# The last block of w_down, loaded in fifteen shares of 15 to 1 rows

## The chip, the core and the metric

The kernel runs on one core of one Trainium2 chip. The time is that of the device, in microseconds (us), for one execution of the whole program; three executions of the kernel before gave a median of 1309.13 us, from 1309.1 to 1309.35. A profile is one further execution, recorded by the hardware: its span runs from the first to the last instruction, and its times count from the start of that span. PE is the matrix engine (its weight loads are listed apart, as PEld), DVE the vector engine, ACT the scalar engine, POOL GpSimd. SP is the engine that issues nearly all transfers, and 16 DMA engines move them.

## What is computed

One decode step of a transformer block for two sequences, all in float32: a layer norm, attention of 32 heads against caches of 8192 keys and values, and a gated feed-forward part (SwiGLU).

```python
h = x + attention(layernorm(x), k_cache, v_cache, wq, wo)   # B=2, H=32, Sk=8192, Dh=128
g = silu(layernorm(h) @ w_gate)                             # D=512, F=1792
u = layernorm(h) @ w_up
h2 = h + (g * u) @ w_down                                   # w_down is 1792 x 512
```

## The kernel before, in words

The two caches are 537 MB of the 565 MB that the core reads, so the program is a long stream of loads with work beside it. SP issues every load in one fixed order, from the list `loads` (loop at line 603): `wq`, then for each of the 32 rounds a tile of keys and a tile of values (8 MB each), then `wo` in two transfers, `w_gate` in one and `w_up` in two, and last `w_down` in five. Before the first transfer into a buffer that was used before, SP waits until the last reader of that buffer is done (`after`, `freed`). `wd_t`, the place of `w_down`, is the buffer of the last value tile, so SP's wait ahead of `w_down` is for the last attention product (line 346). The five `w_down` transfers then follow each other with no wait between them.

`w_down` is loaded with row p of the on-chip tile holding the 14 rows p*14 to p*14+13 of the matrix, one after the other: 14 column blocks of 512 numbers. `WD` cuts these 14 blocks into groups of 4, 4, 3, 2 and 1; each group is one transfer over all 128 partitions with its own semaphore, `wd0` to `wd4`, counted to 16. The last, `wd4`, is 128 rows of 2 KB, 256 KB.

At the end of the program everything hangs on PE: for each of the 14 blocks `c` it does four matmuls (line 583) into the four quarters of the tile `f_ps` (shown as `bank` in the profile), and ahead of the first block of each group it waits for the group's semaphore. A float32 matmul counts as two MATMUL and two LDWEIGHTS rows in the profile, so the group of one block is 8 of each. When the last matmul is done, DVE and ACT each copy half of the result (lines 596 and 597), and SP and ACT each store half (line 610). SP then clears the semaphores and waits for the stores.

Every semaphore is taken one by one with `alone`; `landed` maps a transfer to its semaphore and the count that says that it has arrived, and `wait("tensor", ...)` puts that wait into PE's stream.

Of the kernel before, what the change touches and what calls it, by code (L numbers as in the profile page):

```python
# [9 lines left out]
P = 128  # L10
# [3 lines left out]
class Program:  # L14
# [16 lines left out]
    def wait(self, engine, *points):  # L31
        for s, value in points:
            if self.known[engine].get(s, 0) < value:
                self.known[engine][s] = value
                self.steps[engine].append(lambda e, s=s, v=value: e.wait_ge(s, v))  # L35

    def do(self, engine, fn, sem=None, by=1):

        if sem is None:
            self.steps[engine].append(fn)  # L40
            return None
        self.count[sem] += by
        self.steps[engine].append(lambda e: fn(e).then_inc(sem, by))
        return sem, self.count[sem]
# [8 lines left out]
def decode_block(nc, x, k_cache, v_cache, wq, wo, w_gate, w_up, w_down, out):  # L53
    B, _, D = x.shape
# [4 lines left out]
    FB = F // P  # L59
# [73 lines left out]
    wait, do = g.wait, g.do  # L133
# [6 lines left out]
    def alone(name):  # L140
        return g.sem(name)
# [3 lines left out]
    landed = {}  # L145
    freed = {}
    loads = []
# [43 lines left out]
        ))  # L191
    wd_t = v_last
    WD = ((0, 4), (4, 4), (8, 3), (11, 2), (13, 1))
    for e, (c, n) in enumerate(WD):
        loads.append((
            ("wd", 0), e,
            wd_t[:, c * D : (c + n) * D],
            w_down.rearrange("(p c) m -> p (c m)", p=P)[:, c * D : (c + n) * D],
            alone(f"wd{e}"),
        ))  # L200
    count = {}
    for item, e, dst, src, sem in loads:
        count[sem] = count.get(sem, 0) + 16
# [9 lines left out]
    p0 = do("gpsimd", lambda e: e.memset(ident, 0.0), s_pool)  # L213
# [8 lines left out]
    p0 = do("gpsimd", lambda e: e.memset(sides, 0.0), s_pool)  # L222
# [13 lines left out]
    def layernorm(src, ready):  # L236
        wait("vector", *ready)
        p = do("vector", lambda e: e.bn_stats(stats, src), s_dve)  # L238
        wait("vector", p)
        p = do("vector", lambda e: e.bn_aggr(mv, stats), s_dve)  # L240
        wait("vector", p)
        p = do("vector", lambda e: e.tensor_scalar(ve, mv[:, 1:2], EPS, None, op0=OP.add), s_dve)
        wait("gpsimd", p)
        p = do("gpsimd", lambda e: e.tensor_tensor(rstd, ve, mhalf, op=OP.pow), s_pool)
        wait("vector", p)
        p = do(
            "vector",
            lambda e: e.tensor_scalar(y, src, mv[:, 0:1], rstd, op0=OP.subtract, op1=OP.mult),
            s_dve,
        )  # L250
        normed = p
        wait("tensor", p, ident_done)
        for c in range(DC):
            p = do(
                "tensor",
                lambda e, c=c: e.transpose(yt[:, c, :], y.rearrange("b (p c) -> b c p", c=DC)[:, c, :], ident[:B, :B]),
                s_pe if c == DC - 1 else None,
            )
        return normed, p

    _, p = layernorm(xs, [(x_in, 16)])


    for t, value in (
# [6 lines left out]
        p0 = do("gpsimd", lambda e, t=t, value=value: e.memset(t, value), s_pool)  # L271
    wait("gpsimd", p1)
    p0 = do(
        "gpsimd",
        lambda e: e.affine_select(
            out=place,
            in_=place,
            compare_op=OP.not_equal,
            fill=1.0,
            base=0,  # L280
            pattern=[[-1, 32]],
# [8 lines left out]
    p = do("vector", lambda e: e.tensor_copy(xT, yt), s_dve)  # L290
# [10 lines left out]
    for n, (m, b) in enumerate((m, b) for m in range(0, MQ, 4) for b in range(B)):  # L301
# [3 lines left out]
        for c in range(DC):  # L305
            for k in range(2):
                p = do(
                    "tensor",
                    lambda e, ps=ps, c=c, k=k, m=m, b=b: e.matmul(  # L309
                        ps[HALF[k]],  # L310
                        xb[:, c * B + b, :],
                        wqv[:, c, k, m : m + 4, :],
                        start=(c == 0),
                        stop=(c == DC - 1),
                    ),
# [111 lines left out]
    for i in range(U):  # L427
        m, b = divmod(i, B)
        parts = 2
        n = NJ // parts  # L430
        wait("vector", q_done[m // 4 * B + b])
        for c in range(parts):
# [7 lines left out]
            if i and c == 1:  # L440
                recip(i - 1)
            wait("vector", mult)
            p = do(
                "vector",
                lambda e, kt=kt, s=scores[i % 2][:, c * n : (c + 1) * n]: e.tensor_reduce(s, kt, axis=AX.X, op=OP.add),  # L445
                s_dve,
            )
        freed["k", i] = p
        if i:
# [16 lines left out]
    p = do(  # L466
        "vector",
        lambda e: e.tensor_tensor(
            om,
            oT.rearrange("p h b -> p b h")[:, :, :, None].to_broadcast([P, B, H, NQ]),  # L470
            quarter[:, None, None, :].to_broadcast([P, B, H, NQ]),
            op=OP.mult,
        ),
        s_dve,
    )
    wait("tensor", p)
    for b in range(B):
        p = do(
            "tensor",
            lambda e, b=b: e.matmul(  # L480
                oq_ps[:, b, :], om[:, b].rearrange("p h q -> p (h q)"), fold, start=True, stop=True
            ),
            s_pe if b == B - 1 else None,
        )
    wait("scalar", p)
    p = do("scalar", lambda e: e.activation(oq.rearrange("p c b -> p b c"), oq_ps, AF.Copy), s_act)
    wait("tensor", p, zeroed)
    for c in range(H):
        for e_, (c0, n) in enumerate(WO):
            if c0 == c:  # L490
                wait("tensor", landed[("wo", 0), e_])
        t = c % 4
        p = do(
            "tensor",
            lambda e, c=c, t=t: e.matmul(
                wide[0][32 * t : 32 * t + B, :],
                oq[:, c, :],
                wo_t[:, c * D : (c + 1) * D],
                start=(c < 4),
                stop=(c >= H - 4),  # L500
            ),
# [4 lines left out]
    p = do("scalar", lambda e: e.activation(osb, wide[0], AF.Copy), s_act)  # L506
# [13 lines left out]
    def project_f(first, ps):  # L520
        for c in range(DC):
            for e_, (c0, n) in enumerate(WF):
                if c0 == first + c:
                    wait("tensor", landed[("wf", 0), e_])
            w = wf_t[:, (first + c) * F : (first + c + 1) * F]
            for t in range(4):
                p = do(
                    "tensor",
                    lambda e, c=c, t=t, w=w: e.matmul(
                        ps[32 * t : 32 * t + 32, :],  # L530
                        hT[:, c, :],
                        w[:, t * FQ : (t + 1) * FQ],
                        start=(c == 0),
                        stop=(c == DC - 1),
                    ),
                    s_pe if c == DC - 1 and t == 3 else None,
                )
        return p

    gate, up = wide[1][:, :FQ], wide[0][:, :FQ]  # L540
    p = project_f(0, gate)

    wait("tensor", h1_done)
    for t in range(4):
# [8 lines left out]
    p = do("scalar", lambda e: e.activation(sg, gate, AF.Sigmoid), s_act)  # L553
    wait("vector", p)
    sg_done = do("vector", lambda e: e.tensor_mul(sg, gate, sg), s_dve)
    p = project_f(DC, up)
# [4 lines left out]
    p = do(  # L561
        "vector",
        lambda e: e.tensor_mul(
            gu.rearrange("p (c j) -> p j c", c=FB),
            up.rearrange("p (j c) -> p j c", c=FB),
            sg.rearrange("p (j c) -> p j c", c=FB),
        ),
        s_dve,
    )
    gT = rest[:, D + 2 * FQ : D + 3 * FQ]  # L570
    wait("vector", p)
    p = do("vector", lambda e: e.transpose(gT, gu), s_dve)
# [3 lines left out]
    for c in range(FB):  # L576
        for e_, (c0, n) in enumerate(WD):
            if c0 == c:
                wait("tensor", landed[("wd", 0), e_])
        for t in range(4):  # L580
            p = do(
                "tensor",
                lambda e, c=c, t=t: e.matmul(  # L583
                    f_ps[32 * t : 32 * t + 32, :],
                    gT[:, c * 32 : (c + 1) * 32],
                    wd_t[:, c * D + COLS[t] * P : c * D + (COLS[t] + 1) * P],
                    start=False,
                    stop=(c == FB - 1),
                ),
                s_pe if c == FB - 1 and t == 3 else None,  # L590
            )
# [13 lines left out]
    rows = out.rearrange("b s d -> (b s) d")  # L605
# [55 lines left out]
```

## Time and profile before

| what | value |
|---|---|
| median of three executions | 1309.13 us (1309.1 to 1309.35) |
| span of the profiled execution | 1308.1 us |
| median less span: what lies around the span | about 1.0 us |
| DVE busy | 1131.1 us, 86% |
| PE busy | 433.8 us, 33% |
| ACT busy | 80.7 us, 6% |
| bytes moved | 564.79 MB, mean 432 GB/s |
| first `w_down` transfer issued | 1269.38 us |
| first matmul of the last block | 1305.95 us |

The profiled execution's own time is not listed apart from its span; it is read as the span and the 1.0 us around it. The row of DMA use is in the tenths of each of 40 slices of the span, and the chain of waits follows the work that ended last back from the last instruction, step by step, to what released it. A group row gives an operation, its output and inputs, and how many; the bracket at the end of a timeline row gives the engine's idle time before it and who ended it.

### The profile page before, as it was taken

How to read it: one execution, taken by the hardware profiler on the slowest of the kernel's cores; microseconds unless marked ns; L12 is line 12 of the kernel's file. 1: busy time of each engine (PE TensorE's matmuls, PEld its weight loads, DVE VectorE, ACT ScalarE, POOL GpSimd, SP SyncE). 2: the span in 40 equal slices, each digit the busy share in tenths (PEclk: the TensorE clock that was granted, in tenths of full speed). 3: DMA queues.
4: the chain of work that ended last, by engine and by line, in shares of the span. 5: the costliest groups of instructions: out<-in, count | busy, mean ns of one | idle time of the engine just before them, and what ended most of it. 6: DMA issues, size and time to landing. Idle time of an engine off the chain costs nothing.

```text
span 1308.1 us, 6717 instructions
## 1 busy us (share of the span) xinstructions
PE 433.8 (33%) x2956; PEld 135.8 (10%) x2956; DVE 1131.1 (86%) x246; ACT 80.7 (6%) x272; POOL 3.1 (0%) x15
## 2 busy tenths in 40 slices
PE   3633123333213333312333321333331233332177
PEld 1211001011001011000101100101100010110022
DVE  1999988899888889888889988888988888998841
ACT  0100000000000000000000000000000000000010
POOL 0000000000000000000000000000000000000000
PEclk9866566666556666556666655666655666665578
DMA  9999999999999999999999999999999999999998
GB/s 402 439 439 441 425 423 443 437 431 443 425 441 425 443 423 445 421 445 427 441 439 427 443 425 443 423 441 425 443 423 443 443 425 445 423 443 425 441 418 378
DMA packets 10965, 564.79 MB, mean 432 GB/s; under 512 B 1222, under 2 KB 1226, under 8 KB 1612
## 3 DMA queue, kind: packets, MB, share of 16 engines
q1 hardware_dynamic: 10948, 564.67, 99.7%
q8 instruction: 5, 0.08, 0.0%
q14 instruction: 4, 0.03, 0.0%
q10 hardware_dynamic: 8, 0.01, 0.0%
HBM read 564.66 MB, written 0.00 MB: 432 GB/s over the span
## 4 chain that ended last, share of the span: by engine, by line
DMA 54%; DVE 45%; PE 1%; SPq 0%; issue 0%; DVEq 0%
DMA kslot<-in_A_k_cache_dram 48%; DVE kslot L436 22%; DVE s L445 22%; DMA kslot<-in_A_v_cache_dram 3%; DMA kslot<-in_B_w_down_dram 3%; PE opart L346 1%; DVE gm L389 0%; SPq L603 0%; DVE r L415 0%; PE bank L583 0%; DVE m L453 0%; DVE kslot L596 0%; DVEq L35 0%
## 5 line engine op out<-in xcount | busy, mean ns | idle before, releaser
L436 DVE TENSOR_TENSOR kslot<-kslot,qsb 128x8192 f32<-128x8192 f32 x64 | 555.6, 8681 | 127.9 <-DMA kslot<-in_A_k_cache_dram 127.9
L445 DVE TENSOR_REDUCE s<-kslot 128x64 f32<-128x8192 f32 x64 | 555.2, 8675 | 0.1
L346 PE MATMUL opart<-vslot,pz 128*8 128x512 f32 x1984 | 283.8, 737 | 247.3 <-DMA vslot<-in_A_v_cache_dram 247.3
L338 PE MATMUL bank<-gm,nscale 1*64 1x1 f32 x64 | 11.8, 251 | 359.1 <-DVE gm L389 359.1
L346 PEld LDWEIGHTS opart<-vslot,pz 128*8 128x8 f32 x1984 | 55.1, 103 | 449.9 <-DMA vslot<-in_A_v_cache_dram 249.9
L336 PE MATMUL bank<-ident,m 128*1 128x128 f32 x64 | 18.8, 396 | 168.9 <-DVE m L453 168.9
L338 PEld LDWEIGHTS bank<-gm,nscale 1*64 1x64 f32 x64 | 9.1, 200 | 375.1 <-DVE gm L389 375.1
L358 PE MATMUL bank<-rdiag,osb 128*128 128x2 f32 x256 | 33.7, 254 | 25.7 <-ACT osb L422 25.7
L396 ACT ACTIVATE nb<-bank 128x1 f32<-128x1 f32 x32 | 5.5, 171 | 553.1 <-PE bank L339 553.1
L417 ACT ACTIVATE rdiag<-fold,r 128x8 f32<-128x8 f32 x32 | 9.6, 300 | 484.6 <-DVE r L415 484.6
L358 PEld LDWEIGHTS bank<-rdiag,osb 128*128 128x128 f32 x256 | 31.0, 191 | 55.4 <-ACT osb L422 55.4
L309 PE MATMUL wide<-vslot,osb 128*64 128x512 f32 x128 | 30.3, 638 | 17.2 <-DMA vslot<-in_A_wq_dram 17.2
L341 PE MATMUL bank<-rs,sides 128*128 128x1 f32 x64 | 18.7, 361 | 41.4 <-ACT pz L402 41.4
L402 ACT ACTIVATE pz<-s,nb 64x128 f32<-64x128 f32 x64 | 25.5, 399 | 1.4
L422 ACT ACTIVATE osb<-opart 128x512 f32<-128x512 f32 x32 | 19.1, 597 | 69.6 <-PE opart L346 69.6
L336 PEld LDWEIGHTS bank<-ident,m 128*1 128x1 f32 x64 | 2.7, 81 | 172.4 <-DVE m L453 172.4
L341 PEld LDWEIGHTS bank<-rs,sides 128*128 128x128 f32 x64 | 16.0, 310 | 44.2 <-ACT pz L402 44.2
L309 PEld LDWEIGHTS wide<-vslot,osb 128*64 128x64 f32 x128 | 10.7, 148 | 36.1 <-issue 36.1
L238 DVE BATCH_NORM_STATS2 ln_stats<-attn 2x6 f32<-2x512 f32 x1 | 0.7, 686 | 13.2 <-PE attn L508 13.2
L402 ACT ACTIVATION_READ_ACCUMULATOR pz<-s,nb 64x1 f32 x64 | 11.8, 184 | 0.0
L339 PE MATMUL bank<-gm,nscale 1*64 1x1 f32 x64 | 11.8, 251 | 0.0
L453 DVE TENSOR_REDUCE m<-s 128x1 f32<-128x128 f32 x32 | 9.2, 286 | 1.1
(65 smaller groups left out, 97.3 us busy)
## 6 DMA issues: line engine op xcount, KB each, us to landing
kslot<-in_A_k_cache_dram SPq DMA_DIRECT2D x2, 4096.0 KB, 35.6
vslot<-in_A_wo_dram SPq DMA_DIRECT2D x1, 5120.0 KB, 21.8
kslot<-in_B_w_gate_dram SPq DMA_DIRECT2D x1, 3584.0 KB, 31.6
kslot<-in_B_w_up_dram SPq DMA_DIRECT2D x2, 1792.0 KB, 37.4
vslot<-in_A_wo_dram SPq DMA_DIRECT2D x1, 3072.0 KB, 28.7
kslot<-in_B_w_down_dram SPq DMA_DIRECT2D x2, 1024.0 KB, 31.4
kslot<-in_B_w_down_dram SPq DMA_DIRECT2D x1, 768.0 KB, 33.8
kslot<-in_B_w_down_dram SPq DMA_DIRECT2D x1, 512.0 KB, 34.6
```

The source lines that it names most:

```text
L309: lambda e, ps=ps, c=c, k=k, m=m, b=b: e.matmul(ps[HALF[k]], xb[:, c * B + b, :], wqv[:, c, k, m : m + 4, :], start=(c == 0), stop=(c == D ...
L336: e.matmul(mrow, m1, ident, start=True, stop=True).then_inc(s_pe, 1)
L338: e.matmul(nb_ps[HALF[0]], nscale, gm[:, 0:1], start=True, stop=True)
L339: e.matmul(nb_ps[HALF[1]], nscale, gm[:, 1:2], start=True, stop=True).then_inc(s_pe, 1)
L341: e.matmul(den, sides.rearrange("p w a -> p (w a)"), rs, start=True, stop=True).then_inc(s_pe, 1)
L346: inst = e.matmul(opart[32 * t : 32 * t + 2 * W, :], pz[:, w, :], t_v[:, w * W * DH : (w + 1) * W * DH], start=(w < 4), stop=(w >= NW - 4),)
L358: inst = e.matmul(ot_ps, osb[:, a * DH : (a + 1) * DH], rdiag[:, a::W], start=(a == 0), stop=(a == W - 1))
L402: lambda e, k=k, h=h: e.activation(pz[h, :, k * W : (k + 1) * W], s[h].rearrange("p (w a) -> p w a", a=W), AF.Exp, bias=nb[h], scale=SCALE ...
L417: do("scalar", lambda e: e.activation(rdiag, diag, AF.Copy, scale=r))
L422: do("scalar", lambda e: e.activation(osb, opart, AF.Copy), s_act_pe)
L436: mult = do("vector", lambda e, kt=kt, qb=qb: e.tensor_tensor(kt, kt, qb, op=OP.mult), s_dve)
L445: lambda e, kt=kt, s=scores[i % 2][:, c * n : (c + 1) * n]: e.tensor_reduce(s, kt, axis=AX.X, op=OP.add),
```

## The change

The last group of `WD` is no longer one transfer. Its 128 partitions are cut into fifteen consecutive shares, `SHARES`, of 15, 14, 13, 12, 11, 10, 10, 9, 8, 7, 6, 5, 4, 3 and 1 partitions. Each is a transfer of its own, with its own semaphore `wdl0` to `wdl14`. PE waits for all fifteen ahead of the last block. The first four groups, the bytes and their places are as before.

```diff
     WD = ((0, 4), (4, 4), (8, 3), (11, 2), (13, 1))
-    for e, (c, n) in enumerate(WD):
+    wd_src = w_down.rearrange("(p c) m -> p (c m)", p=P)
+    for e, (c, n) in enumerate(WD[:-1]):
         loads.append((
             ("wd", 0), e,
             wd_t[:, c * D : (c + n) * D],
-            w_down.rearrange("(p c) m -> p (c m)", p=P)[:, c * D : (c + n) * D],
+            wd_src[:, c * D : (c + n) * D],
             alone(f"wd{e}"),
         ))
+    SHARES = (15, 14, 13, 12, 11, 10, 10, 9, 8, 7, 6, 5, 4, 3, 1)
+    assert sum(SHARES) == P
+    p0 = 0
+    for e, n in enumerate(SHARES):
+        rows = slice(p0, p0 + n)
+        p0 += n
+        cols = slice(WD[-1][0] * D, FB * D)
+        loads.append((("wd", 0), len(WD) - 1 + e, wd_t[rows, cols], wd_src[rows, cols], alone(f"wdl{e}")))
...
     for c in range(FB):
         for e_, (c0, n) in enumerate(WD):
             if c0 == c:
-                wait("tensor", landed[("wd", 0), e_])
+                for e_ in (e_,) if c < FB - 1 else range(e_, e_ + len(SHARES)):
+                    wait("tensor", landed[("wd", 0), e_])
```

On SP, the end of the stream of loads before; `kslot0` is the buffer that holds `w_down`, the sizes are partitions x numbers, and the waits are named by semaphore:

```order
L603 DMA kslot1<-in_B_w_up_dram 128x3584 x2
L603 DMA kslot0<-in_B_w_down_dram 128x2048 [waits pe]
L603 DMA kslot0<-in_B_w_down_dram 128x2048
L603 DMA kslot0<-in_B_w_down_dram 128x1536
L603 DMA kslot0<-in_B_w_down_dram 128x1024
L603 DMA kslot0<-in_B_w_down_dram 128x512
L610 DMA out_0_dram<-kslot1 2x256 [waits res]
```

And the same place on SP now, from the fourth `w_down` transfer on (shares of 4, 3 and 1 partitions and the store follow):

```order
L615 DMA kslot0<-in_B_w_down_dram 128x1024
L615 DMA kslot0<-in_B_w_down_dram 15x512
L615 DMA kslot0<-in_B_w_down_dram 14x512
L615 DMA kslot0<-in_B_w_down_dram 13x512
L615 DMA kslot0<-in_B_w_down_dram 12x512
L615 DMA kslot0<-in_B_w_down_dram 11x512
L615 DMA kslot0<-in_B_w_down_dram 10x512 x2
L615 DMA kslot0<-in_B_w_down_dram 9x512
L615 DMA kslot0<-in_B_w_down_dram 8x512
L615 DMA kslot0<-in_B_w_down_dram 7x512
L615 DMA kslot0<-in_B_w_down_dram 6x512
L615 DMA kslot0<-in_B_w_down_dram 5x512
```

One issue has become fifteen, in the same place, ahead of the store of the result; nothing else on SP has moved.

On PE, the end of the program before (`bank1` is `f_ps`):

```order
L583 MATMUL bank1<-kslot0,kslot1 32x128 [waits wd2]
L583 MATMUL bank1<-kslot0,kslot1 32x128 x11
L583 MATMUL bank1<-kslot0,kslot1 32x128 [waits wd3]
L583 MATMUL bank1<-kslot0,kslot1 32x128 x7
L583 MATMUL bank1<-kslot0,kslot1 32x128 [waits wd4]
L583 MATMUL bank1<-kslot0,kslot1 32x128 x3
```

And now:

```order
L595 MATMUL bank1<-kslot0,kslot1 32x128 [waits wd2]
L595 MATMUL bank1<-kslot0,kslot1 32x128 x11
L595 MATMUL bank1<-kslot0,kslot1 32x128 [waits wd3]
L595 MATMUL bank1<-kslot0,kslot1 32x128 x7
L595 MATMUL bank1<-kslot0,kslot1 32x128 [waits wdl8,wdl7,wdl9,wdl6,wdl10,wdl5,wdl11,wdl4,wdl12,wdl3,wdl13,wdl2,wdl14,wdl1,wdl0]
L595 MATMUL bank1<-kslot0,kslot1 32x128 x3
```

The matmuls stand as they did; ahead of the last block one wait has become fifteen. In the built program the fourteen added ones stand in seven wait instructions of two semaphores each, and the fifteenth, for `wdl0`, is on the first weight load itself.

## The prediction

> **What bounds the kernel now.** I read the page's DMA row first, then the chain that ended last, then the last microseconds. The page:
>
> ```profile
> span 1308.1 us, 6717 instructions
> DMA  9999999999999999999999999999999999999998
> DMA 54%; DVE 45%; PE 1%; SPq 0%; issue 0%; DVEq 0%
> ```
>
> The 16 DMA engines are never idle until the last slice, so the loads set the length; the change touches 256 KB of 565 MB, at the very end. Only what happens after the last bytes are asked for can move. The chain in order of time, its last steps (start, length, what):
>
> ```profile
> 1269.38 0.33 SPq L603
> ...
> 1270.69 34.58 DMA kslot<-in_B_w_down_dram
> 1305.27 0.04 issue
> 1305.32 1.10 PE bank L583 x24
> 1306.42 0.02 issue
> 1306.44 0.28 DVE kslot L596
> ```
>
> The chain enters PE with the fourth group (two blocks), issued at 1270.69 and landed at 1305.27. The last transfers are issued some 34 us ahead of their landing. The timeline shows where the fifth comes in:
>
> ```profile
> 1304.05 0.86 PE L583 MATMUL bank<-kslot 128*32 128x128 f32 x24 [0.77 <-DMA kslot<-in_B_w_down_dram]
> 1305.32 0.38 PEld L583 LDWEIGHTS bank<-kslot 128*32 128x32 f32 x16 [0.67 <-DMA kslot<-in_B_w_down_dram]
> 1305.95 0.16 PEld L583 LDWEIGHTS bank<-kslot 128*32 128x32 f32 x8 [0.26 <-DMA kslot<-in_B_w_down_dram]
> 1306.44 0.28 DVE L596 COPY kslot<-bank 64x128 f32<-64x128 f32 x1 [5.67 <-PE bank L583]
> 1306.75 0.34 SPq L610 DMA_DIRECT2D out_dram<-kslot  x1
> ```
>
> The weight loads of the last block begin at 1305.95, after 0.26 us without work because the fifth transfer was not there. Those 0.26 us are all that the transfer costs now: had it landed long before, PE would still begin at 1305.32 with the fourth group and reach the last block at about 1305.69. **The most that this change can win is therefore 0.26 us, 0.02%.** A measurement of this kernel can tell about 0.2%, 2.6 us, from no change.
>
> **Why a transfer lands late.** DMA use at the end, in windows of 0.1 to 0.3 us (the last two columns are the mean busy share of the 16 engines and the rate):
>
> ```profile
> core 0: us, PE busy (x) PEld busy (x) DVE busy (x) ACT busy (x) POOL busy (x), PEclk, DMA share, GB/s
> 1303.50:1303.80 0.30, 0.00 (x0) 0.00 (x0) 0.00 (x0) 0.00 (x0) 0.00 (x0) 1.00 1.02 403
> 1304.20:1304.40 0.20, 0.20 (x12) 0.20 (x9) 0.00 (x0) 0.00 (x0) 0.00 (x0) 1.00 0.33 133
> 1304.60:1304.90 0.30, 0.30 (x12) 0.04 (x4) 0.00 (x0) 0.00 (x0) 0.00 (x0) 1.00 0.33 130
> 1305.00:1305.10 0.10, 0.00 (x0) 0.00 (x0) 0.00 (x0) 0.00 (x0) 0.00 (x0) 1.00 0.37 143
> 1305.40:1305.50 0.10, 0.10 (x8) 0.10 (x12) 0.00 (x0) 0.00 (x0) 0.00 (x0) 1.00 0.11 41
> 1305.60:1306.00 0.40, 0.40 (x20) 0.14 (x12) 0.00 (x0) 0.00 (x0) 0.00 (x0) 1.00 0.00 0
> ```
>
> Until 1303.8 all sixteen are busy; from 1304.2 to 1305.1 the share is 0.33 to 0.37, some six of sixteen (0.375); the last stops by 1305.6. So most engines finish about 1304.2, a group of about six runs up to 1.4 us behind, and the slowest decides every landing. Dealing out the last rows unevenly could help if the late engines get fewer. The rows do not say which engines these are.
>
> **Row time.** Groups three to five reach PE at 1304.05, 1305.32 and 1305.95. Between the last two lies the fifth group, 8 rows of 2 KB on each engine if 128 rows fall evenly on 16: 0.63 us, 0.079 us a row. The fourth, of 4 KB rows, took 1.27 us, just twice that, so what a transfer adds besides its rows is about nothing when it is queued well ahead (twice 0.63 is 1.26). Bounds for that addition in a small transfer: below, 0.00 by these two; above, 0.36 us, the time from the last busy DMA engine (before 1305.6) to PE's start at 1305.95, if an engine had to see each arrival confirmed before its next row. I take a value near the lower bound, 0.01, since the sequence of five queued transfers is the nearest row; the upper one is a rival.
>
> **The change, term by term.** *Where the rows go.* A transfer of n rows seems to use n engines, one row each, for n below 16. The only small load in the trace, x (2 rows of 2 KB), seen in slices of 4 ns:
>
> ```profile
> GB/s 0 0 0 0 0 0 0 0 0 0 0 0 0 0 0 0 512 512 0 0 0 0 0 0 0 0 0 0 0 0 0 0 0 0 0 1 1 0 0 0
> DMA packets 4, 0.00 MB, mean 26 GB/s; under 512 B 2, under 2 KB 2, under 8 KB 4
> q10 hardware_dynamic: 4, 0.00, 7.0%
> ```
>
> Its two packets of 2 KB start within 8 ns of each other, and one lasts about 80, so they ran on two engines. Estimate from this: fifteen shares give the engine that takes part in all of them 15 rows, then 14, 14, 13, 12, 11, 10, 9, 8, 7, 5, 4, 3, 2, 1 and 0, where each had 8. [...]
>
> An early engine with 15 rows ends at about 1304.2 + 7 x 0.09 = 1304.8, still ahead of the late ones. The slowest late engine moves by between -8 and +7 rows: -0.63 to +0.55 us. The gain stops at 0.26, because the fourth group is what is late next. If late engines were spread at random over the stair, the slowest two or three would hardly all stand low; I take +0.2 us for the landing.
>
> *PE.* Seven wait instructions are added; the trace has five like them:
>
> ```profile
> L35 PEldq EVENT_SEMAPHORE  x5: 51/51/51, 1.5 to 1299.7; - x5
> ```
>
> Queued behind them on PE are the last 8 weight loads and matmuls, and DVE, ACT and the store wait for those. Seven by 51 ns, with a step between, are 0.36 to 0.42 us if the share that comes last is in the first of them; nothing if it is in the last. Waits already met could also be passed while PE waits for others. I take +0.2 us.
>
> *SP.* Fourteen more issues:
>
> ```profile
> L603 SPq DMA_DIRECT2D kslot<-in_B_w_down_dram x5: 327/428/2540, 1269.4 to 1271.2; - x5
> 0.74 0.54 ACTq L212 DMA_DIRECT2D xs<-in_A_x_dram  x1
> 1251.18 0.80 SPq L603 DMA_DIRECT2D vslot<-in_A_wo_dram  x2
> vslot<-in_A_wo_dram SPq DMA_DIRECT2D x1, 5120.0 KB, 21.8
> vslot<-in_A_wo_dram SPq DMA_DIRECT2D x1, 3072.0 KB, 28.7
> kslot<-in_B_w_gate_dram SPq DMA_DIRECT2D x1, 3584.0 KB, 31.6
> ```
>
> At 0.43 us (SP's) to 0.54 us (x, which went to few engines) they take 6.0 to 7.6 us of SP, which waits until 1306.75 for its next work, the store. They begin at 1271.2 and the last row's turn comes at about 1303.2, so 25 us cover them. But the fifth issue took 2.54 us, to 1273.7: something was full. The first wo transfer landed at 1251.18 + 21.8 = 1273.0, just before. If the limit counts rows waiting for an engine, the shares fit as rows drain: the busiest engine gets 15 rows and 15 completions where it had 8 and 1, 21 more; 8 rows and a completion leave with the second wo transfer (landed about 1251.55 + 28.7 = 1280.3), 9 more with w_gate (1257.1 + 31.6 = 1288.7), the rest by about 1291, 12 us ahead of need. **Cost nothing**, as long as that is the limit.
>
> *Code.* The added instructions could bring one more code fetch into the tail:
>
> ```profile
> q8 instruction: 1, 0.02, 2.1%
> ```
>
> That is the window from 1303.2 to 1306: one fetch, 2.1% of 16 engines over 2.8 us, 0.94 us of one engine. Seven instructions on PE and fourteen on SP may or may not start another; 0 to +0.94 us, taken as 0.
>
> The sum: landing +0.2, PE +0.2, SP 0, code 0: +0.4 on the profiled 1308.1, or 1309.5 beside the median of 1309.13. The bounds: -0.26 with nothing added, and 0.55 + 0.42 + 0.94 = +1.9.
>
> **Rivals.** *The stair fits the late engines* (they are those with few rows): then the landing gains its 0.26 and PE's waits give back some; 1308.9 to 1309.2. Six late engines against six places with 5 to 0 rows speak for it; nothing shows that they are the same six. Within 0.2% too.
>
> *The limit counts transfers, not rows.* When the fifth issue stood still, nine were in flight (2 of wo, 3 of w_gate and w_up, 4 of w_down), and it went on 0.3 us after the oldest had landed, less its own 0.43. Then each share waits for one landing: the first nine by that of the fourth group, 1305.27, so that the ninth is issued by about 1306.0 and the last six, at 0.43, by 1308.6. From the start of the final store's issue (1306.75) to the end of the span are 1.35 us; so the last share lands at 1308.2 + 1.35 = 1309.5 instead of 1305.9: +3.6, **1312.7**, slower. It decides if the cap is below some 20 in flight. Against it: the stop ended at 1273.7, 0.7 us after the landing where an issue takes 0.43; while the slowest engine's next row of the second wo transfer, 0.9 us (7.3 us by 8) after its last of the first at about 1272.7, ends at 1273.6, just ahead of it. Rows fit better.
>
> *Small transfers pay per piece.* If each share costs an engine the 0.36 above, the busiest has 15 x 0.44 = 6.6 us from about 1303.2, then 0.36: 1310.2 instead of 1305.95, +4.2, **1313.3**. Against it: the queued transfers of four and two KB rows show no such part. [...]
>
> *The shares do not spread* (128 rows on one engine: 10 us, about 1317): x speaks against it.
>
> **How the numbers follow.** Forecast 0.66, fitting stair 0.20: both within 0.2%. Transfers counted 0.07, per piece 0.05, not spread 0.01: slower. Faster by over 2.6 us has no mechanism here: 0.01. So faster 0.01, same 0.86, slower 0.13. The range takes the bounds of the first two cases, 1309.13 - 0.26 and + 1.9, with 0.1 for scatter below: 1308.7 to 1311.0; the slower rivals are the part left out.
>
> **What would show it.** Right: SP's fifteen issues end before 1292; PE's wait ahead of the last block is within half a microsecond of 0.26; DMA use falls in another shape after 1303.9 but ends by about 1306.2. Transfers counted: issues still running after 1300 and a store that waits for SP. Per piece: DMA share low but not zero for several us after 1305. Code: a second q8 packet in the window from 1303. Wrong altogether if the time moves by more than 2 us with none of these.

## The result, and the profile after

| | before | after |
|---|---|---|
| median, 12 executions each | 1309.40 us (1309.1 to 1309.66) | 1311.84 us (1311.45 to 1312.44) |
| ratio to before, 95% interval | | 1.002 (1.0012 to 1.0028) |
| span of the profiled execution | 1308.1 us | 1310.5 us |

The change costs 2.4 us. That is just under the 0.2% bound of the prediction, but the two sets of executions do not touch, and 1311.84 lies outside the range of 1308.7 to 1311.0. The spans differ by 2.34 us, so the traces hold it. Three executions in what follows (one of e5, the profiled one of e10, one of before beside r0, e1, e2 and e5) took 150 to 440 us longer than the others; the medians leave them out, and e17 repeats e10 for its trace.

The page of after:

```profile
span 1310.5 us, 6738 instructions
DMA  9999999999999999999999999999999999999998
DMA 52%; DVE 45%; SPq 2%; PE 1%; issue 0%; DVEq 0%
```

Nothing of the stream is seen to change; SP's queue enters the chain with 2%. The chain of after in order of time, its last steps (start, length, what):

```profile
1289.29 1.02 SPq L615
1290.31 0.04 issue
1290.36 17.45 DMA kslot<-in_B_w_down_dram
1307.81 0.35 issue
1308.15 0.62 PE bank L595 x8
1308.78 0.02 issue
1308.80 0.28 DVE kslot L608
```

Before, the last landing in the chain was that of the fourth group, at 1305.27; now it is that of a share, at 1307.81, though SP issued it at 1290.3, 17 us ahead. Behind it stand 0.35 us in which PE works through its waits. The timeline of after:

```profile
1305.47 0.38 PEld L595 LDWEIGHTS bank<-kslot 128*32 128x32 f32 x16 [0.83 <-DMA kslot<-in_B_w_down_dram]
1308.12 0.19 PEld L595 LDWEIGHTS bank<-kslot 128*32 128x32 f32 x8 [2.28 <-issue]
1308.15 0.60 PE L595 MATMUL bank<-kslot 128*32 128x128 f32 x8 [2.04 <-DMA kslot<-in_B_w_down_dram]
1308.80 0.28 DVE L608 COPY kslot<-bank 64x128 f32<-64x128 f32 x1 [8.11 <-PE bank L595]
```

PE's idle time ahead of the last block was 0.26 us and is 2.28 us. Its eight weight loads and matmuls then take 0.68 us to the copy (1308.12 to 1308.80) where they took 0.49. The window of after around them shows why; the third number from the right is the clock that PE is granted, as a share of full speed:

```profile
1308.00:1308.80 0.80, 0.60 (x8) 0.19 (x8) 0.00 (x0) 0.00 (x0) 0.00 (x0) 0.67 0.00 0
```

The trace's records of this clock have it fall from 1.0 to 0.5 at 1308.27, within the block. In before it is 1.0 from 1294.36 to 1308.01, and the last matmul is done by 1306.44.

Now the question is whether the bytes come late. The use of the 16 DMA engines in 40 slices of 1303 to 1308 us, 0.125 us each, in tenths; first before, then after:

```profile
DMA  9999999944334243321000000000000000001000
```

```profile
DMA  8967927552443333311000000000000000000000
```

Both rows fall below a tenth after the 19th slice: the bytes end at nearly the same place. The same in windows, after (the last two columns are DMA share and GB/s):

```profile
1305.40:1305.90 0.50, 0.43 (x16) 0.38 (x16) 0.00 (x0) 0.00 (x0) 0.00 (x0) 1.00 0.06 21
1305.90:1306.40 0.50, 0.22 (x8) 0.00 (x0) 0.00 (x0) 0.00 (x0) 0.00 (x0) 1.00 0.00 0
```

After 1305.9 no DMA engine moves data, and the last landing is at 1307.81. So the time does not pass in moving bytes but between the last byte and the word that it has arrived. The trace's records of the semaphores show how that word comes: each engine that takes part in a transfer adds one when its part is done. The last of these additions for each share of after, in us, with the number of engines that took part (it is the number of rows, as the prediction had it from x):

```
share (engines)   0(15)   1(14)   2(13)   3(12)   4(11)   5(10)   6(10)
last addition     1305.61 1305.80 1305.99 1306.17 1306.36 1306.54 1306.72
share (engines)   7(9)    8(8)    9(7)    10(6)   11(5)   12(4)   13(3)   14(1)
last addition     1306.89 1307.07 1307.26 1307.44 1307.63 1307.81 1307.16 1306.11
last row of w_down moved: 1305.89     last addition: 1307.81
```

Shares 0 to 12 step by 0.17 to 0.19 us: one engine, with 13 rows, that reports one share after another. Its rows need 0.086 us each, and it has moved them all by 1305.89. The reports fall behind the rows by some 0.1 us a share until they lag by 1.92 us; before, the one report lagged by 0.32 (last row 1305.58, landing 1305.90). They do not start level: the last row of the fourth group is moved at 1304.78 and its landing is at 1305.43, 0.65 us behind, where before it was 0.34 behind (1304.93 and 1305.27).

In the records of the DMA engines each row of a share is followed by a packet of 4 bytes, one for each report, that takes 9 ns. The last of these packets ends at 1305.90, just behind the last row. So the engines work off the reports at the pace of the rows; it is their arrival that comes 0.18 us apart.

The 2.34 us between the two traces, by place: last row 0.31 later, reports behind it 1.60 more (1.26 from the thirteen shares, 0.33 the lag that the fourth group has already), PE's waits 0.27, PE's slower last block 0.18, the rest -0.02.

### The profile page after: what moved, and what is told of

It reads as the page before. It is cut to its first block, busy times and chain, and to the rows that moved or that the text cites. A ratio compares the mean times of both kernels' runs of the same rounds, so it can differ in the third digit from the quotient of the medians.

```text
span 1310.5 us, 6738 instructions
## 1 busy us (share of the span) xinstructions
PE 433.4 (33%) x2956; PEld 135.6 (10%) x2956; DVE 1131.1 (86%) x246; ACT 80.7 (6%) x272; POOL 3.1 (0%) x15
## 4 chain that ended last, share of the span: by engine, by line
DMA 52%; DVE 45%; SPq 2%; PE 1%; issue 0%; DVEq 0%
DMA kslot<-in_A_k_cache_dram 48%; DVE kslot L447 22%; DVE s L456 22%; DMA kslot<-in_A_v_cache_dram 3%; SPq L615 2%; DMA kslot<-in_B_w_down_dram 1%; PE opart L357 1%; DVE gm L400 0%; DVE r L426 0%; PE bank L595 0%; DVE m L464 0%; DVE kslot L608 0%; DVEq L35 0%
```

## The experiments

The expectations use these letters. **C**: an engine's reports (completions) follow each other some 0.18 us apart, which is slower than short rows. **R**: the stair puts 13 to 15 rows on some engine where each had 8. **S**: a small transfer pays a price wherever it stands in the stream. Later: **P**, shares of neighbouring partitions slow what lands beside them (crowding); **N**, the number of transfers counts; **G**, only the added issue and the shifted program code count.

| label | last block loaded as | median | before beside it | ratio, 95% |
|---|---|---|---|---|
| r0_changed_again | as in after | 1312.08 | 1309.27 | 1.002 (1.001 to 1.003) |
| e1_one_semaphore | 15 shares, one semaphore | 1311.89 | 1309.27 | 1.0019 (1.0009 to 1.0028) |
| e2_eight_by_16 | 8 shares | 1310.82 | 1309.27 | 1.0011 (1.0001 to 1.002) |
| e5_stair_of_four | 60, 40, 20, 8 | 1309.92 | 1309.27 | 1.0005 (0.9995 to 1.0015) |
| e3_four_by_32 | 4 shares | 1310.16 | 1309.35 | 1.0006 (0.9996 to 1.0015) |
| e4_two_by_64 | 2 halves | 1310.17 | 1309.35 | 1.0006 (0.9997 to 1.0015) |
| e6_eight_by_16_one_semaphore | 8 shares, one semaphore | 1310.92 | 1309.35 | 1.0011 (1.0002 to 1.0021) |
| e7_shares_first_one_semaphore | 15 shares, ahead of the other groups | 1311.75 | 1309.35 | 1.0019 (1.001 to 1.0029) |
| e9_two_by_64_interleaved | every 2nd partition | 1309.53 | 1309.43 | 0.9999 (0.999 to 1.0008) |
| e16_four_by_32_interleaved | every 4th | 1309.40 | 1309.31 | 0.9995 (0.9979 to 1.0012) |
| e10_eight_interleaved_one_semaphore | every 8th, one semaphore | 1310.93 | 1309.43 | 1.0012 (1.0003 to 1.0021) |
| e17_eight_interleaved_again | the same | 1311.14 | 1309.31 | 1.0006 (0.9988 to 1.0024) |
| e11_fourth_group_in_two | whole; fourth group in two | 1309.23 | 1309.43 | 0.9998 (0.9989 to 1.0007) |
| e8_three_blocks_8_by_16 | last 3 blocks, 8 shares | 1312.92 | 1309.43 | 1.0027 (1.0017 to 1.0036) |
| e12_three_blocks_interleaved | the same, every 8th | 1312.52 | 1309.26 | 1.0022 (1.0013 to 1.0032) |
| e13_whole_block_first | whole, ahead of the other groups | 1309.63 | 1309.26 | 1.0002 (0.9993 to 1.0012) |
| e14_eight_interleaved_first | every 8th, ahead | 1311.01 | 1309.26 | 1.0012 (1.0002 to 1.0022) |
| e15_eight_by_16_first | 8 shares, ahead | 1310.63 | 1309.26 | 1.001 (1.0 to 1.0019) |

All edits below are against after, except that of e7, which is against before.

### The waits and the stair: r0, e1, e2, e6, e5

> The changed kernel once more, as the measure for the others on this chip. Expected +2.2 to +2.6 us against the kernel before. By its first trace: data of the last shares gone by 1306.0, the last share counted as landed at 1307.81, PE's last block at 1308.12 instead of 1305.95.

Measured 2.8 us above before, more than expected, where the first comparison had 2.4. The reports step as in after, by 0.17 to 0.20 us, and the last landing is at 1308.01.

One semaphore for all shares, and one wait of PE:

```diff
+    wdl = alone("wdl")
-        loads.append((("wd", 0), len(WD) - 1 + e, wd_t[rows, cols], wd_src[rows, cols], alone(f"wdl{e}")))
+        loads.append((("wd", 0), len(WD) - 1 + e, wd_t[rows, cols], wd_src[rows, cols], wdl))
...
-                for e_ in (e_,) if c < FB - 1 else range(e_, e_ + len(SHARES)):
+                for e_ in (e_,) if c < FB - 1 else (e_ + len(SHARES) - 1,):
```

> Fifteen shares as in the change, but all on one semaphore, and PE waits once, for the full count of 240. If PE's chain of waits costs what its trace shows (last landing 1307.81, last block 1308.12, where one wait takes 0.05), this wins 0.25 to 0.3 us of the change's loss, so +2.1 against before, and the last landing stays near 1307.8. If the waits were the main cost, +0 to +0.5. If the separate semaphores slow the landings, the landing itself comes early.

Measured 1311.89 beside 1312.08 on the same chip: the separate waits are worth some 0.2 us, no more, and the loss is 2.6 us where 2.1 were expected. The two sets of executions overlap, so the 0.2 us rest on the traces. The timeline of e1 shows PE starting 0.04 us after the last landing (1307.63) and still late:

```profile
1307.67 0.20 PEld L596 LDWEIGHTS bank<-kslot 128*32 128x32 f32 x8 [2.00 <-DMA kslot<-in_B_w_down_dram]
1308.39 0.28 DVE L609 COPY kslot<-bank 64x128 f32<-64x128 f32 x1 [8.03 <-PE bank L596]
```

The block again takes 0.72 us, so that part does not hang on the number of semaphores. It does not hang on the length of the wait either: e6 and e17 (below) have PE idle for 1.07 and 1.12 us ahead of the last block, and the block takes 0.72 and 0.49 us. In e17:

```profile
1307.80 0.16 PEld L595 LDWEIGHTS bank<-kslot 128*32 128x32 f32 x8 [1.12 <-DMA kslot<-in_B_w_down_dram]
1308.29 0.28 DVE L608 COPY kslot<-bank 64x128 f32<-64x128 f32 x1 [7.26 <-PE bank L595]
```

It goes with the granted clock. Where the clock stays at 1.0 over a last group of one block, the block takes 0.49 to 0.52 us (before, e3, e5, e9, e11, e16, e17); where the clock has fallen to 0.5 before or within it, 0.68 to 0.74 us (after, r0, e1, e2, e6). In after the fall comes 13.65 us after the rise, as it does in before. What makes it fall is not shown by any run.

Equal shares, without the stair:

```diff
-    SHARES = (15, 14, 13, 12, 11, 10, 10, 9, 8, 7, 6, 5, 4, 3, 1)
+    SHARES = (16, 16, 16, 16, 16, 16, 16, 16)
```

> Eight shares of 16 rows, one row on each of the 16 engines and one completion for each: every engine has 8 rows as before, but 8 completions instead of 1, and no stair. Theory C (an engine's completions go out one after another, about 0.18 us each, slower than rows of 0.086): the slowest engine lands 8 x 0.18 = 1.44 us after its fourth group instead of 0.63, +0.8, and PE's three added wait instructions +0.1 to 0.3: +0.9 to +1.1 us against before. Theory R (the loss is the stair: the late engine was given 13 rows): no loss here, -0.1 to +0.2. [...]

> Eight shares of 16 as before, on one semaphore with one wait on PE. The run with eight semaphores had its last landing at 1306.98 and PE's last block at 1307.09, so PE's waits cost it only 0.06 beyond the single wait's 0.05. Theory C: landing again near 1307.0, last block 0.05 later; within 0.1 us of the eight semaphores' time (+1.3 to +1.6 against before). If separate semaphores were what makes completions slow, the landing comes near 1306.

1310.82, and 1310.92 with one semaphore: 1.6 us above before, with 8 rows on every engine as there. R alone falls. The time is also above the 0.9 to 1.1 us that C gave for e2: its last landing is 1.08 us later than before's, not 0.8, and the granted clock adds 0.25 in the last block (0.74 instead of 0.49). In e2 the last additions of the eight shares step by 0.19 to 0.22 us (1305.57, .77, .99, 1306.19, .39, .59, .79, .98), while the last row was moved at 1305.50. C's step holds for equal shares too, and the fifteen shares cost about 1 us more because 13 reports stand on the slowest engine instead of 8.

```diff
-    SHARES = (15, 14, 13, 12, 11, 10, 10, 9, 8, 7, 6, 5, 4, 3, 1)
+    SHARES = (60, 40, 20, 8)
```

> A stair again, but of four transfers of 60, 40, 20 and 8 partitions: if these go to 15, 10, 10 and 8 engines, engines 0 to 7 get 11 rows, 8 and 9 get 10, 10 to 14 get 4, and 15 none; four completions at most on an engine. Theory C: completions hide behind rows (4, 4, 2 and 1 rows at 0.08 between them), so only 3 rows more on the late low engine, +0.24, and little for PE's waits: +0.2 to +0.6. Theory R with a high price for rows given to the late engine: 3 of the 5 rows added by the change, +1.1. Theory S: four transfers, +0.6.

1309.92, 0.65 above before: just above C's range, near the 0.6 of S, and well below the 1.1 of R. On how many engines the shares of 60, 40 and 20 rows land is not shown here; 15, 10 and 10 were my assumption.

### Fewer, larger shares: e3, e4

`SHARES` is `(32, 32, 32, 32)` in e3, 64 KB a share, and `(64, 64)` in e4; nothing else is changed.

> Four shares of 32 rows: 2 rows and one completion on each engine per share. Theory C as the first runs left it (completions go out one per 0.18 to 0.20 us on an engine, beside the rows and not in their way): 2 rows take 0.165, so the last landing is at most 0.1 to 0.2 us later than before's 1305.90; PE's wait +0.1. In all +0.1 to +0.4 us. Theory C-added (a completion adds 0.1 us to its engine's rows): +0.3 at the landing, +0.4 to +0.5 in all. Theory S (each transfer of 64 KB or less pays a fixed price, 1.1 us for 7 more in the run with 8): 3 more, +0.5.

> Two shares of 64 rows: 4 rows (0.32 us) and one completion on each engine per share. Theory C: a completion of 0.18 to 0.20 hides behind 4 rows, last landing within 0.1 us of before's 1305.90, one more wait on PE; +0.0 to +0.2 us. If issuing the added transfer brought its own price (a further code fetch near 1280 us stood in all four traces of changed kernels and not in that of before), +0.3 or more and the fourth group's landing later than 1305.27.

Both took 0.8 us more than before: a miss for C, which has next to nothing to give where each report has two or four rows to hide behind (0.17 and 0.35 us). In e4 it was the fourth group, untouched by the edit, that landed late: 1306.05 instead of 1305.27. Something slowed the bytes.

### Shares ahead of the other groups: e7

The loop over `SHARES` stands ahead of the loop over `WD[:-1]`, with one semaphore:

```diff
-    for e, (c, n) in enumerate(WD):
...
+    wdl = alone("wdl")
+    for e, n in enumerate(SHARES):
...
+    for e, (c, n) in enumerate(WD[:-1]):
```

> The fifteen shares are issued ahead of the four large groups instead of behind them, on one semaphore; the bytes, the stair and the 128 completions are the same. Theory C: the completions drain while the 3.75 MB of the large groups move, and nothing at the end waits for them; what is left is the stair, 13 rows instead of 8 for the late engine 3, 5 x 0.086 = 0.43 on every later landing, so the fourth group lands at 1306.2 to 1306.5 instead of 1305.90 for the whole, and PE then has 24 matmul rows to go instead of 8: in all +0.6 to +1.0 us against before, at least 1 us better than the shares last (+2.6 with one semaphore +2.4). If the price sits in the transfers wherever they stand (S), the loss stays at +2 or more.

1311.75: another miss for C. All rows of the shares were moved by 1298.4 and the last report came at 1300.3, yet the fourth group landed at 1307.44. The loss is not only a backlog of reports at the program's end. S says so, but not why.

### Which partitions a share takes: e9, e10, e16, e17

A share takes every second (fourth, eighth) partition instead of neighbours; sizes and numbers of transfers stay:

```diff
-        rows = slice(p0, p0 + n)
-        p0 += n
+        rows = slice(e, P, len(SHARES))
```

> Two transfers of 64 partitions again, but of every second partition (0, 2, 4 .. and 1, 3, 5 ..) instead of the lower and the upper half. [...] Theory C (completions of one engine's transfers go out one after another, whatever the partitions): as with the halves, 1310.0 to 1310.3, fourth group near 1306.0.

> Four transfers of every fourth partition, each with its semaphore, in place of the four of 32 neighbouring partitions that took 1310.16. Theory N (the number of transfers, so of completions, sets the loss; with two it is hidden, with eight 1.5 us): 1309.8 to 1310.3, as with neighbouring partitions. Theory P (neighbouring partitions set the loss up to where completions take over at eight): 1309.3 to 1309.7.

1309.53 for two and 1309.40 for four: the 0.8 us are gone, though issues, semaphores, waits and rows are as many as in e4 and e3. The windows show what they were. First e4 (neighbouring halves), then e9 (interleaved halves):

```profile
1303.70:1304.30 0.60, 0.00 (x0) 0.00 (x0) 0.00 (x0) 0.00 (x0) 0.00 (x0) 1.00 0.89 191
```

```profile
1303.70:1304.30 0.60, 0.00 (x0) 0.00 (x0) 0.00 (x0) 0.00 (x0) 0.00 (x0) 1.00 1.06 406
```

Then e3 (neighbouring quarters) and e16 (interleaved quarters):

```profile
1303.70:1304.30 0.60, 0.01 (x1) 0.01 (x1) 0.00 (x0) 0.00 (x0) 0.00 (x0) 1.00 0.76 164
```

```profile
1303.70:1304.30 0.60, 0.60 (x24) 0.53 (x24) 0.00 (x0) 0.00 (x0) 0.00 (x0) 1.00 0.41 160
```

Read share and rate together. A DMA engine that is busy all the time moves some 24 GB/s (406 over 16 x 1.06 = 24; 160 over 16 x 0.41 = 24). With neighbouring partitions the engines are busy too (0.89 and 0.76 of the time) and move 13 GB/s each (191 over 16 x 0.89, 164 over 16 x 0.76). A busy engine here is one that is held up. Every row that lands in that time is stretched, those of the fourth group as well: its 4 KB rows take 0.26 us on average in e3 and e4 from 1303.5 to 1304.5, and 0.159 in e9 and e16. Reports come later too: those of the third and fourth group, one for eight rows, are 0.66 to 0.78 us behind their last row in e3 and e4, and 0.32 to 0.34 in e9, e16 and before. Even a 16 KB fetch of program code in that stretch takes 1.28 to 1.30 us instead of 0.93.

> Eight transfers of 16 partitions with one semaphore, each of every eighth partition. Theory P: the time falls from the 1310.9 of the eight blocks of neighbouring partitions to 1309.4 to 1309.9, and the completions of one engine come about 0.09 us apart like its rows. Theory C: no change, 1310.7 to 1311.1, with completions 0.17 to 0.20 us apart.

> The eight interleaved shares with one semaphore once more, for an undisturbed profile: 1310.7 to 1311.2 as before. If the shares stretch whatever lands beside them, the 4 KB rows of the fourth group take more than 0.159 us while the first shares land, and the 16 KB code fetch near the end more than 0.93. Theory C alone: the rows keep their 0.159 us and only the completions lag.

Eight interleaved shares cost as much as eight of neighbours, 1310.93 and 1311.14: within the range of C for e10. In e17's trace both things stand side by side. The 4 KB rows take 0.27 us from 1304.0 to 1304.5 and the code fetch 1.23; and the last row is moved at 1306.18, the last report comes at 1307.76, with 0.17 and 0.19 us between the last three. Its windows:

```profile
1303.70:1304.30 0.60, 0.00 (x0) 0.00 (x0) 0.00 (x0) 0.00 (x0) 0.00 (x0) 1.00 1.08 345
1304.30:1304.90 0.60, 0.21 (x8) 0.21 (x12) 0.00 (x0) 0.00 (x0) 0.00 (x0) 1.00 0.48 120
1305.90:1306.40 0.50, 0.09 (x4) 0.09 (x8) 0.00 (x0) 0.00 (x0) 0.00 (x0) 1.00 0.07 25
```

120 over 16 x 0.48 is 16 GB/s an engine: crowded, though the partitions are no neighbours. P as I had worded it ("neighbouring") falls here. The runs give no rule for it: every second and every fourth partition lose nothing (e9 and e16, 1309.53 and 1309.40), while halves and quarters of neighbours (13 GB/s an engine in e4 and e3) and every eighth partition (16 in e17) are crowded. What sets these apart was not shown. Both arrangements of eight shares that were run lose 1.5 to 1.8 us, so there the choice of partitions is not separated from N, by which the many reports themselves would hold up the engines; for two and four shares N is ruled out by e9 and e16.

### An added issue alone: e11

```diff
-    WD = ((0, 4), (4, 4), (8, 3), (11, 2), (13, 1))
+    WD = ((0, 4), (4, 4), (8, 3), (11, 1), (12, 1), (13, 1))
-    SHARES = (15, 14, 13, 12, 11, 10, 10, 9, 8, 7, 6, 5, 4, 3, 1)
+    SHARES = (128,)
```

> The last block is one transfer of 128 partitions again; the fourth group is cut by columns instead, into two transfers of one block and 128 partitions each. Like the two halves it has one SP issue, one semaphore and one PE wait more than before. Theory G (an issue more moves the program's code and its late fetch, and that costs the time, not the size of the shares): 1310.0 to 1310.3 like the halves. Theories C and P: no transfer is small or crowded, 1309.3 to 1309.6.

1309.23: a transfer more, of 128 partitions, costs nothing. G falls.

### Long rows: e8, e12

The fourth and fifth group become one of three blocks (6 KB a row), loaded by eight shares with one semaphore, of neighbours in e8 and of every eighth partition in e12:

```diff
-    WD = ((0, 4), (4, 4), (8, 3), (11, 2), (13, 1))
+    WD = ((0, 4), (4, 4), (8, 3), (11, 3))
```

> The last group holds three blocks (6 KB a row, 0.23 us of an engine) and is loaded by eight transfers of 16 partitions with one semaphore; the fourth group is gone into it. Theory C with the completion beside the next row: completions of one engine come 0.23 to 0.25 us apart, right behind the rows, and the last is within 0.4 us of the last row. Theory C with the completion added to the row: 0.31 to 0.36 us apart. PE has three blocks to do after the landing instead of one, about 1.0 us more, so 1310.3 to 1310.7 by the first and 1311.0 to 1311.6 by the second.

> The last three blocks by eight transfers of 16 partitions with one semaphore, as in the run that took 1312.9, but each of every eighth partition. Theory P: the 6 KB rows take 0.23 us throughout instead of 0.37 to 0.42 while many engines run, the 16 KB code fetch near the end 0.93 us instead of 1.21, and the time falls to 1310.9 to 1311.7. Theory C alone: no change, 1312.6 to 1313.2.

1312.92 and 1312.52. Both are misses for every theory's number: the time is above both ranges for e8, and e12 is near the end named for C alone, although its rows are far from untouched. The windows of before, e8 and e12 in the same stretch:

```profile
1303.10:1303.70 0.60, 0.18 (x8) 0.00 (x0) 0.00 (x0) 0.00 (x0) 0.00 (x0) 1.00 0.97 386
```

```profile
1303.10:1303.70 0.60, 0.00 (x0) 0.00 (x0) 0.00 (x0) 0.00 (x0) 0.00 (x0) 1.00 0.96 174
```

```profile
1303.10:1303.70 0.60, 0.23 (x10) 0.00 (x0) 0.00 (x0) 0.00 (x0) 0.00 (x0) 1.00 1.01 184
```

All 16 engines are busy and the rate is less than half, 174 and 184 GB/s instead of 386. With rows this long the reports keep up: the last comes 0.58 us (e8) and 0.42 us (e12) after the last row. So here the loss is the rate (last row 1306.77 and 1307.44, 1.2 and 1.9 later than before), and PE's three blocks, 1.58 us from weight load to copy instead of 0.49 for one. Of these some 0.65 are the granted clock of 0.5: the same 24 matmul rows take 0.93 us in e13, at 1.0.

### What the shares cost ahead of longer rows: e13, e14, e15

As e7, with `SHARES = (128,)` in e13, eight interleaved shares in e14 and eight of neighbours in e15.

> The last block is one transfer of 128 partitions with one semaphore again, and it is loaded ahead of the other four groups, as the fifteen shares were in the run that took 1311.75. It is that run's control: PE has two blocks and one waiting block to do after the last landing instead of one, about 0.4 us more. By all theories 1309.6 to 1310.0; what the fifteen shares cost in that place is then the difference.

> The last block as eight shares of every eighth partition, one semaphore, ahead of the other four groups. Theory P (crowding of neighbouring partitions is what costs where long rows follow; completions lag but don't hold the rows behind): as the whole block in that place, 1309.6 to 1310.1. Theory C with completions that hold the engine's next rows: about 0.8 us more, 1310.4 to 1310.9.

> The same with eight shares of 16 neighbouring partitions. Theory P: 0.5 to 1.0 us more than the whole block in that place (the first group's rows behind them stretch on every engine, as in the run with the fifteen shares), 1310.2 to 1311.0. Theory C: the same as with interleaved partitions.

The order by itself costs little (1309.63). Against that control the shares cost 1.4 us (e14) and 1.0 us (e15), and e7's fifteen, each against its own before, 2.0 us. The windows in which the shares land, e13, then e14, e15 and e7:

```profile
1296.60:1297.60 1.00, 0.69 (x8) 0.29 (x12) 0.00 (x0) 0.00 (x0) 0.00 (x0) 1.00 1.07 449
```

```profile
1296.60:1297.60 1.00, 0.00 (x0) 0.00 (x0) 0.00 (x0) 0.00 (x0) 0.00 (x0) 1.00 0.89 285
```

```profile
1296.60:1297.60 1.00, 0.03 (x4) 0.04 (x5) 0.00 (x0) 0.00 (x0) 0.00 (x0) 1.00 1.05 340
```

```profile
1296.60:1297.60 1.00, 0.00 (x0) 0.00 (x0) 0.00 (x0) 0.00 (x0) 0.00 (x0) 1.00 1.05 322
```

By the busy engine (rate over 16 x share) it is 26 GB/s in e13 and 20, 20 and 19 in the others: a quarter of the rate is gone, for some 3 us, the 8 KB rows of the next group taking 0.40 to 0.43 us in this window instead of 0.309. e14 lies above both its ranges (P had these rows untouched); e15 lies within that of P. The reports have long caught up when the last group lands: in e14 it lands 0.35 us after its last row (1306.80, 1307.15), as a whole transfer does. So in this place the reports' lag costs nothing and the lower rate costs all of it: the last row is moved 1.67 us later than in e13 (1306.80 against 1305.13), and the spans differ by 1.7. The DMA engines bound the stream to its end here, and a lower rate some 8 us ahead of the end was still paid in full.

No version here beats before by more than its measurement can tell.

## Why the prediction was wrong, point by point

**What bounds the kernel; the most to win.** Right as far as the runs go: no kernel won more than the 0.26 us, nor any of it measurably. The landing of the last block still sets the end. That the 2.4 us stay under the 2.6 that were to count as no change is luck, since the sum had +0.4. By its last sign, a move of more than 2 us with none of the rivals' marks, the prediction was wrong altogether.

**The addition of a small transfer** is the step that failed. I bounded it by 0.00 and 0.36 us and took 0.01, from two queued transfers whose landings fitted "rows only". Those have 8 rows of 0.079 us or more for each report, and a report of about 0.18 us hides behind them. The change gives every row its own report. What had to be sized was the larger of the rows and a report, not their sum: 0.18 instead of 0.086 us a share (in e9, with four rows to a report, the reports come 0.31 us apart, about the time of the rows). On the slowest engine that is 13 x 0.18 = 2.4 us after the fourth group, where the whole transfer took 0.63. Of the 1.91 us by which the landing moved, 1.26 are this; 0.31 are the later last row and 0.33 a lag that the fourth group's report has already. The added 0.1 us a share lay inside my bounds, but the range was built on 0.01, taken from rows that could not show it.

**The rival "per piece"** named the mechanism, at 0.44 us a share, 15 shares and 1313.3, and I gave it 0.05. Measured are 0.18 and 13. The sign by which I meant to know it was wrong too: DMA use is not low for several us after 1305, it is 0.06 from 1305.4 to 1305.9 and then zero, while the reports come until 1307.81: a report that is waited for does not count as busy. The row that speaks for it is the landing far behind the last byte. Size alone does not decide: the shares of 2 to 30 KB lost 2.4 us, but shares of 64 KB cost nothing when interleaved (e16) and 0.8 us when not (e3), and e8's shares of 96 KB lose more than 1 us in their rows.

**The stair.** I took +0.2 us for late engines with many rows. The last row moved by 0.31: right in kind and near in size. The slowest engine had 13 rows, so the rival "the stair fits the late engines" is refuted: followed from share to share, the six late engines have 14, 13, 11, 10, 7 and 1 rows. How the 0.31 us divide between five more rows (0.43 by 0.086) and the crowding of that stretch is not separated.

**PE's waits.** I took +0.2; the trace has 0.27, and e1 beside r0 0.19. Right. Not foreseen: the later block runs into a lower granted clock and takes 0.68 us instead of 0.49.

**SP** was right. Its row in after:

```profile
L615 SPq DMA_DIRECT2D kslot<-in_B_w_down_dram x19: 252/1012/3111, 1269.3 to 1291.3; - x19
```

Nineteen issues, held up to 3.1 us each, are over by 1291.6, before the 1292 that I had named, and with all nineteen in flight, since the first of them lands at 1299.40. A cap of nine transfers, on which that rival rests, is refuted.

**Code** was right as a cost of nothing: one fetch of 8 KB more (five instead of four on that queue), at 1280 us; e11 has it too and loses nothing.

**Not in the prediction at all:** the crowding. In after it shows as well. Its window, to be read against the 386 GB/s at 0.97 of before:

```profile
1303.10:1303.70 0.60, 0.00 (x0) 0.00 (x0) 0.00 (x0) 0.00 (x0) 0.00 (x0) 1.00 0.79 266
```

266 over 16 x 0.79 is 21 GB/s an engine instead of 25, and the 4 KB rows take 0.18 us. With two or four shares it is the whole loss (e9 and e16 lose nothing). With fifteen it can be no more than the 0.31 us of the last row and the 0.33 us by which the fourth group's report lags already; why it cost less here than in e4 was not tested.

## What to carry to other kernels

Cutting a queued transfer cost nothing here as long as each part gave every engine two rows or more (0.17 us) and took every second or fourth partition: four interleaved quarters were free, eight shares of one row per engine cost 1.5 to 1.8 us. Look for the time between the last byte and the last landing, which DMA use does not show (0.00 in after while the last 1.9 us of reports came in), and divide GB/s by DMA share: a busy engine that moves half its bytes (13 instead of 24 GB/s in e4) is being held up. A price that was read from large transfers says nothing of small ones, if something can hide behind the large ones' rows.

## What the runs showed that I had not expected

- An engine's reports come 0.17 to 0.22 us apart (after, e2, e17), even when it is the only one left, while its rows go at 0.086 us. They come behind the rows (last row 1305.89, last addition 1307.81), and no run shows what the 0.18 us are spent on.
- Shares that take only some of the partitions can halve the rate of all 16 engines (174 and 184 GB/s at DMA shares of 0.96 and 1.01 in e8 and e12), and other transfers' rows and code fetches slow with them: 16 KB of code took 1.23 to 1.30 us instead of 0.93 in e3, e4 and e17.
- Why six DMA engines run late: if each engine's packets are followed back to back through the trace of before, six are 0.9 to 1.6 us behind from the moment on at which code was fetched through them, four by one fetch of 16 KB (0.88 to 0.96 us, at 44, 53, 1265 and 1293 us) and two by two fetches of 8 KB each (0.31 us by their own records, at 211, 233, 849 and 955). The landings agree: of the 16 additions for one tile two come 1.7 and 1.9 us after the first at 63 us, and six come 1.1 to 1.7 us after it at 1297 us. In this stream without a gap nobody catches up, so a fetch in the first 60 us is still in the last landing.
